# One plan for all engines, and a first block of tokens that takes all twelve weight columns in one pass

## The chip, the core and the metric

The kernel runs on one core of a Trainium2 chip. The core has a matrix engine (TensorE, PE in the profile, with its weight loads as PEld), a vector engine (VectorE, DVE), an engine for functions and copies (ScalarE, ACT), a general engine (GpSimd, POOL) and an engine whose queue issues the DMAs (SyncE, SP). Each works through its own queue in order and waits for the others by semaphores. SBUF is the memory on the chip; matmuls write into eight banks of PSUM. The metric is the device time of one execution in microseconds.

## The reference

Three layers in a row, in float32, on 4 x 768 = 3072 tokens of 384 channels (8 heads of 48). First a gated linear attention, then a product of two projections, then a mixture of four experts:

```python
f = 1.0 / (1.0 + np.exp(-f_logit))
for t in range(S):                       # S = 768, for each batch and head
    state = f[..., t, :, None] * state + k[..., t, :, None] * v[..., t, None, :]
    y[..., t, :] = q[..., t, :] @ state
x = ((y @ w_a) * (y @ w_b)) @ w_out      # 384 -> 1536 -> 384
p = domain_probs / (domain_probs.sum(-1, keepdims=True) + 1e-09)
out = sum(p[:, e:e + 1] * (np.maximum(x @ w1[e], 0.0) @ w2[e]) for e in range(4))
```

The weights `w_a`, `w_b` and `w_out` arrive as float64; all else is float32.

## The kernel before

`phase_a` (line 132) does attention and the second layer, `phase_b` (line 508) the experts. A third part, `general`, is a fallback for inputs outside the limits that `flags` watch; it does not run here.

**Attention** goes in 24 steps of 128 tokens for one batch: step `s` is piece `s // 4` of batch `s % 4`, and four steps make one block of 512 tokens. A step loads f, k, q and v (`a_load`), turns the gates into running products R (`a_exp`, `a_scan`), scales q and k by them (`a_hat`), transposes k (`a_trans`), forms scores and masks them (`a_scores`), and adds up outputs and the state for the step four later (`a_out`). For the first eight steps (`EARLY`, line 31) 1/R comes from Ln and Exp on ScalarE with a correction; for the others from four reciprocals on VectorE (`a_inv`). In the early steps one of the two masks is a copy on ScalarE and a select on GpSimd. The outputs are split into a rounded part and a remainder, `xT`, so that a float32 product is three fast matmuls.

**Weights of the second layer**: 18 units of 128 x 768 numbers, three for every two of the twelve columns (128 wide) of the hidden layer: `w_a` and `w_b` of one column, `w_out` of two, the two projections of the other column. As float64 they arrive as pairs of 32-bit words, 768 KB each (`fetch_w`). `to_f32` (line 97) makes float32 of the words: one pass of ScalarE (line 103) and six of VectorE (lines 104 to 116), the first of them a clamp. `split` then rounds a weight on ScalarE and leaves the remainder to GpSimd.

**The second layer** goes in units, one column for one block of tokens: `half` twice (nine matmuls each), a copy of the first half, the product of both on VectorE, split in two parts, and `outp`, the last product, which adds nine matmuls into three banks. In the first eight units (`WHOLE`) the product and the weight are not split, and `outp` is six instructions of the slower full form. From unit `LATE` = 20 VectorE makes the remainders, before that GpSimd. `outp` stands one unit behind. The first two columns of the first block are done in halves of 256 tokens.

**The order.** Units run over columns 0 to 8 for block 0, the same for block 1, then columns 9 to 11 for block 0 and for block 1 (`H1` = 9, line 459), then all twelve for blocks 2 to 5. Each block's three banks are emptied into `x2raw` at the end of a part; the second part's are added to it there. Attention and conversions are strung between the units by hand (`attn_to`, `conv_to`, from line 403), with fractions of a list of operations due by a unit. The framework's scheduler may still move instructions of one engine, except those that `kept` pins, which are matmuls of blocks 2 to 5. `busy` (line 177) writes filler matmuls on a tile of zeros, 104 in all, between the matmuls of the first four steps.

Of the kernel before, what the change touches and what calls it, by code (L numbers as in the profile page):

```python
# [21 lines left out]
C = 128  # L22
# [8 lines left out]
EARLY = 2 * B  # L31

SLOTS = 11
FREE = 3 * B
LEAD = 2
OUTPOS = 4
AHEAD = 2
GRP = 2
BUSY = (8, 10, 8, 6)
H1 = 9  # L40
NSUB = 2
CA = 2
FRAC = 0.4
WHOLE = 8
LATE = 20
LIMIT = float(2.0 ** 60)
# [6 lines left out]
def gla_moe_moe_kernel(ctx: ExitStack, tc, qkf, vv, wab, wout, w12, probs, gq, gv, gp, out):  # L53
# [12 lines left out]
    def bank(tag, bufs=None, name=None):  # L66

        i = turn.get(tag, 0)
        turn[tag] = i + 1
        return banks8[WHERE[tag][i % len(WHERE[tag])]]  # L70
# [9 lines left out]
    flags = const.tile([128, NSTEP, 3], F32, tag="flags", name="flags")  # L80
    junk = const.tile([128, 1, 128], BF16, tag="junk", name="junk")
# [15 lines left out]
    def to_f32(raw, w=None):  # L97
# [5 lines left out]
        nc.scalar.activation(out=mag, in_=high.bitcast(F32), func=AF.Abs)  # L103
        nc.vector.tensor_scalar(out=mag, in0=mag, scalar1=F64_ZERO, scalar2=F64_INF, op0=ALU.max, op1=ALU.min)
        mag_i, val_i = mag.bitcast(U32), val.bitcast(U32)
        nc.vector.tensor_scalar(
            out=mag_i, in0=mag_i, scalar1=5, scalar2=2, op0=ALU.logical_shift_left, op1=ALU.logical_shift_right
# [24 lines left out]
    def phase_a(actx):  # L132
        ws = actx.enter_context(tc.tile_pool(name="ws", bufs=1))
# [4 lines left out]
        w_f, raws = {}, {}  # L138
# [3 lines left out]
        w_pair = [None]  # L142


        def w_fetch(u):
            f, i = 2 * (u // 3), u % 3
            raws[u] = fetch_w(wout[f // 2] if i == 1 else wab[f + i // 2])

        def w_ready(u):
            f, i = 2 * (u // 3), u % 3  # L150
            raw = raws.pop(u)
            if i == 1:
                dst = wo_all[:, f:f + 2].rearrange("p f c -> p (f c)")
                if wide:
                    to_f32(raw, dst)
                else:
                    nc.scalar.copy(out=dst, in_=raw)
                return
            f += i // 2
            w = to_f32(raw) if wide else raw  # L160
            if f == 0:
                w_pair[0] = wts.tile([128, 2, 2, 2 * DM], F32R, tag="x", name="w01", bufs=1)
            t = w_pair[0][:, f] if f < 2 else wts.tile([128, 2, 2 * DM], F32R, tag="w", name="w")
            split(nc.gpsimd, t[:, 0], t[:, 1], w)
            w_f[f] = t.rearrange("p a (i k c) -> p a i k c", i=2, k=KC)


        T, st_t, xT = {}, {}, {}

        fixed = [False]  # L170

        def kept(ins):

            if fixed[0]:
                tc.keep_in_program_order(ins)

        def busy(n):

            if n:
                b = bank("o")  # L180
                for _ in range(n):
                    nc.tensor.matmul(b, junk[:, 0], junk.to_broadcast([128, 4, 128]), start=True, stop=True)
# [4 lines left out]
        def a_load(s):  # L187
            t = {}
            early = wts.tile([128, 3, 4, C], F32, tag="w", name="qkf") if s < B else None
            for i, name in ((2, "f"), (1, "k"), (0, "q")):  # L190
                t[name] = slot(name) if early is None else early[:, i]
                nc.sync.dma_start(out=t[name], in_=qkf[s, i])
            t["v"] = slot("v").rearrange("p j c -> p (j c)") if early is None else v_early[:, s * 512:(s + 1) * 512]
            t["v"] = t["v"].rearrange("p (h e) -> p h e", h=H)
            nc.sync.dma_start(out=t["v"], in_=vv[s])
            T[s] = t

        def a_exp(s):
            u = T[s]["f"]
            nc.scalar.activation(out=u, in_=u, func=AF.Exp, scale=-1.0)  # L200
            nc.scalar.activation(out=u, in_=u, func=AF.Identity, bias=1.0)
            nc.scalar.activation(out=cap[:, :, 0:1], in_=u[:, :, 0:1], func=AF.Copy)
            T[s]["R"] = slot("R")

        def a_scan(s):

            u, R = T[s]["f"], T[s]["R"]
            flat = [x.rearrange("p j c -> p (j c)") for x in (R, u, cap)]
            nc.vector.tensor_tensor_scan(  # L209
                out=flat[0], data0=flat[1], data1=flat[2], initial=1.0, op0=ALU.mult, op1=ALU.min  # L210
            )

        def a_inv(s, j):
            if s >= EARLY:
                nc.vector.reciprocal(out=T[s]["f"][:, j], in_=T[s]["R"][:, j])  # L215

        def a_hat(s):

            t = T[s]
            R, q, k, p = t.pop("R"), t["q"], t["k"], t.pop("f")  # L220
            end = slice(C - 1, C)
            pe = at.tile([128, 4, 1], F32, tag="pe", name="pe", bufs=3)
            t["pe"] = pe
            j1 = at.tile([128, 4, C], BF16, tag="j", name="j")
            if s >= EARLY:
                nc.gpsimd.tensor_tensor(out=k, in0=k, in1=R, op=ALU.mult)  # L226
                nc.scalar.activation(out=j1, in_=q, func=AF.Square, accum_out=flags[:, s, 1:2])
                nc.vector.tensor_reduce(out=flags[:, s, 0:1], in_=R[:, :, C - 1], axis=AX.X, op=ALU.max)
                nc.vector.tensor_tensor(out=q, in0=q, in1=p, op=ALU.mult)
                nc.vector.tensor_copy(out=pe, in_=p[:, :, end])  # L230
            else:
                nc.scalar.activation(out=p, in_=R, func=AF.Ln)
                nc.scalar.activation(out=p, in_=p, func=AF.Exp, scale=-1.0)
                nc.gpsimd.tensor_tensor(out=k, in0=k, in1=R, op=ALU.mult)
                nc.scalar.activation(out=j1, in_=q, func=AF.Square, accum_out=flags[:, s, 1:2])
                nc.vector.tensor_reduce(out=flags[:, s, 0:1], in_=R[:, :, C - 1], axis=AX.X, op=ALU.max)
                nc.vector.scalar_tensor_tensor(out=q, in0=q, scalar=-1.0, in1=p, op0=ALU.mult, op1=ALU.mult)
                nc.gpsimd.tensor_tensor(out=R, in0=R, in1=p, op=ALU.mult)
                nc.vector.scalar_tensor_tensor(out=q, in0=R, scalar=-2.0, in1=q, op0=ALU.add, op1=ALU.mult)  # L239
                nc.vector.scalar_tensor_tensor(  # L240
                    out=pe, in0=R[:, :, end], scalar=-2.0, in1=p[:, :, end], op0=ALU.add, op1=ALU.mult
                )
            j2 = at.tile([128, 4, C], BF16, tag="j", name="j")
            nc.scalar.activation(out=j2, in_=k, func=AF.Square, accum_out=flags[:, s, 2:3])

        def a_trans(s):

            t = T[s]
            if s // B == NC - 1:
                return  # L250
            kps = bank("k")
            for j in range(4):
                kept(nc.tensor.transpose(kps[:, j * C:(j + 1) * C], t["k"][:, j], ident))
            if s < B:
                busy(BUSY[1])
            t["kt"] = slot("kt")
            nc.scalar.copy(out=t["kt"].rearrange("p j c -> p (j c)"), in_=kps)

        def a_scores(s):
            t = T[s]  # L260
            q, k = t["q"], t.pop("k")
            sps = [bank("s"), bank("s")]
            for j in range(4):
                for h in range(2):
                    r = 64 * h
                    kept(nc.tensor.matmul(  # L266
                        sps[h][:, j * C:(j + 1) * C], k[r:r + D, j], q[r:r + D, j], start=True, stop=True
                    ))
            if s < B:
                busy(BUSY[2])  # L270
            t["s"] = []
            for h in range(2):
                m = slot("ss")
                if h and s < EARLY:
                    nc.scalar.copy(out=m.rearrange("p j c -> p (j c)"), in_=sps[h])
                    nc.gpsimd.affine_select(
                        out=m, in_=m, compare_op=ALU.is_ge, fill=0.0, base=0, pattern=[[0, 4], [1, C]],
                        channel_multiplier=-1,
                    )
                    t["s"].append(m)  # L280
                    continue
                nc.vector.tensor_tensor(
                    out=m,
                    in0=sps[h].rearrange("p (j c) -> p j c", j=4),
                    in1=mask.rearrange("p (o c) -> p o c", o=1).to_broadcast([128, 4, C]),
                    op=ALU.mult,
                )
                t["s"].append(m)

        def a_out(s):  # L290
# [32 lines left out]
            if s < B:  # L323
                busy(BUSY[3])
# [478 lines left out]
```

## Time and profile before

| | |
|---|---|
| median of 3 runs | 1416.17 us (1415.77 to 1416.61) |
| the profiled execution | 1415.95 us |
| its span, first to last instruction | 1414.2 us |
| PE busy in the span | 1381.6 us, 98%, 7599 instructions |
| DVE busy | 583.2 us, 41%, 880 instructions |
| ACT busy | 392.9 us, 28% |
| POOL busy | 191.3 us, 14% |

The page's slices show the engines unevenly loaded: forty slices of 35 us, each digit the busy share in tenths. DVE stands at 7 to 9 for the first five slices and at 2 for the last twenty-odd; PE is at 7 and 8 in the first three and at 9 after them. A share over the whole span says little here; the views are read by stretch. Times in timelines are counted from the start of the span.

### The profile page before, as it was taken

What the parts mean: (1) busy time and instruction counts of PE and PEld (TensorE: products, weight loads), DVE (VectorE), ACT (ScalarE), POOL (GpSimd) and SP (SyncE); (2) the same over time, 40 slices, a digit from 0 to 9 for tenths busy, and PEclk for the clock granted to TensorE, in tenths of its full rate; (3) what the DMA queues carried; (4) which work ended last, traced back from release to release, by engine and by line L of the source; (5) the groups of instructions that cost most, each with busy time, mean ns of one, the idle gap of its engine ahead of it and who ended that gap; (6) DMA issues with size and microseconds to landing.
All of it is one profiled execution on the core that took longest, in us unless ns stands there. A gap on an engine that the chain in (4) does not pass through costs nothing.

```text
span 1414.2 us, 18060 instructions
## 1 busy us (share of the span) xinstructions
PE 1381.6 (98%) x7599; PEld 1190.7 (84%) x7599; DVE 583.2 (41%) x880; ACT 392.9 (28%) x733; POOL 191.3 (14%) x128
## 2 busy tenths in 40 slices
PE   7889999999999999999999999999999999999998
PEld 4676787888888878889999989999989999989997
DVE  7899716856565654432222222222222222222222
ACT  6453334433333324341111211111311112111111
POOL 4334431100000002360000310000300002100000
PEclk9889999999999999999999999999999999999999
DMA  6544101222121101200000200000200001000001
GB/s 232 168 156 147 53 0 44 67 65 57 32 66 45 56 17 35 68 23 0 1 1 0 68 23 1 0 1 1 89 1 0 1 0 45 1 23 23 23 23 47
DMA packets 28168, 60.27 MB, mean 43 GB/s; under 512 B 4016, under 2 KB 9392, under 8 KB 28080
## 3 DMA queue, kind: packets, MB, share of 16 engines
q1 hardware_dynamic: 28080, 59.05, 13.3%
q8 instruction: 61, 1.00, 0.3%
q14 instruction: 27, 0.22, 0.0%
HBM read 51.95 MB, written 4.72 MB: 40 GB/s over the span
## 4 chain that ended last, share of the span: by engine, by line


## 5 line engine op out<-in xcount | busy, mean ns | idle before, releaser
L545 PE MATMUL bank<-w,h 128*128 128x384 f32 x2304 | 411.3, 335 | 0.0
L545 PEld LDWEIGHTS bank<-w,h 128*128 128x128 f32 x2304 | 402.8, 188 | 5.0
L527 PE MATMUL bank<-x,w 128*128 128x512 f32 x1728 | 404.8, 390 | 0.0
L527 PEld LDWEIGHTS bank<-x,w 128*128 128x128 f32 x1728 | 323.3, 188 | 65.2
L530 DVE SCALAR_TENSOR_TENSOR h<-bank,h 128x512 fp32r<-128x512 f32 x192 | 132.7, 691 | 533.1 <-ACT h L529 533.1
L358 PE MATMUL bank<-xT,w 128*128 128x512 f32 (+1 forms) x1332 | 319.1, 390 | 3.4 <-DVE ab L494 1.6
L358 PEld LDWEIGHTS bank<-xT,w 128*128 128x128 f32 x1332 | 246.2, 190 | 57.7 <-DVE ab L494 2.4
L529 ACT ACTIVATE h<-bank 128x512 fp32r<-128x512 f32 x192 | 114.9, 598 | 616.0 <-PE bank L527 516.7
L376 PE MATMUL bank<-hl,wo 128*128 128x512 f32 x594 | 148.9, 394 | 1.6 <-DVE hl L122 1.1
L122 POOL TENSOR_TENSOR w<-raw,w 128x768 fp32r<-128x768 f32 x32 | 59.0, 1844 | 575.6 <-ACT w L121 573.6
L376 PEld LDWEIGHTS bank<-hl,wo 128*128 128x128 f32 x594 | 109.9, 188 | 27.3 <-DVE hl L122 1.8
L494 DVE TENSOR_TENSOR ab<-bank,a 128x512 f32<-128x512 f32 x66 | 45.0, 682 | 132.7 <-PE bank L358 132.7
L121 ACT CAST hl<-ab 128x512 fp32r<-128x512 f32 x66 | 40.9, 620 | 83.5 <-DVE ab L494 83.5
L555 DVE SCALAR_TENSOR_TENSOR acc<-bank,pr,acc 128x384 f32<-128x384 f32 x72 | 39.5, 610 | 58.6 <-PE bank L545 58.6
L486 ACT COPY a<-bank 128x512 f32<-128x512 f32 (+1 forms) x74 | 42.1, 569 | 70.0 <-PE bank L358 70.0
L122 DVE TENSOR_TENSOR hl<-ab,hl 128x512 fp32r<-128x512 f32 x54 | 49.4, 914 | 28.6 <-ACT hl L121 28.6
L215 DVE RECIPROCAL f<-R 128x128 f32<-128x128 f32 x64 | 57.6, 926 | 0.7
L226 POOL TENSOR_TENSOR k<-k,R 128x512 f32<-128x512 f32 x16 | 22.0, 1373 | 265.6 <-DVE R L209 247.0
L121 ACT CAST wo<-wo_all 128x384 fp32r<-128x384 f32 x66 | 33.9, 515 | 40.0 <-PE bank L376 39.2
L122 DVE TENSOR_TENSOR wo<-wo_all,wo 128x384 fp32r<-128x384 f32 x54 | 34.4, 637 | 19.1 <-ACT wo L121 19.0
L121 ACT CAST w<-raw 128x768 fp32r<-128x768 f32 x32 | 26.8, 837 | 44.7 <-PE bank L545 30.8
L266 PE MATMUL bank<-q,k 48*128 48x128 f32 x320 | 25.6, 296 | 6.5 <-DVE q L239 5.8
(106 smaller groups left out, 773.0 us busy)
## 6 DMA issues: line engine op xcount, KB each, us to landing
raw<-in_w_dram SPq DMA_DIRECT2D x32, 384.0 KB, 3.0
raw<-in_wab_dram SPq DMA_DIRECT2D x12, 768.0 KB, 4.9
f<-in_qkf_dram SPq DMA_DIRECT2D x20, 256.0 KB, 2.7
k<-in_qkf_dram SPq DMA_DIRECT2D x20, 256.0 KB, 2.7
q<-in_qkf_dram SPq DMA_DIRECT2D x20, 256.0 KB, 2.8
v<-in_v_dram SPq DMA_DIRECT2D x20, 256.0 KB, 3.0
raw<-in_wout_dram SPq DMA_DIRECT2D x6, 768.0 KB, 4.4
out_dram<-acc SPq DMA_DIRECT2D x24, 192.0 KB, 1.9
```

Of the source, the lines that this page charges most:

```text
L121: nc.scalar.copy(out=hi, in_=x)
L122: engine.tensor_tensor(out=lo, in0=x, in1=hi.bitcast(F32), op=ALU.subtract)
L215: nc.vector.reciprocal(out=T[s]["f"][:, j], in_=T[s]["R"][:, j])
L358: kept(nc.tensor.matmul(p, l, r, start=m == 0, stop=m == len(ops) - 1))
L376: kept(nc.tensor.matmul(banks[m][:, o:o + n], w[:, a, m * 128:(m + 1) * 128], hl[:, b], start=f == fs[0] and q == 0 and o == 0, stop=f == ...
L486: nc.scalar.copy(out=a, in_=pa)
L494: nc.vector.tensor_tensor(out=ab, in0=pb, in1=a, op=ALU.mult)
L527: nc.tensor.matmul(p, l, r, start=i == 0, stop=i == len(ops) - 1)
L529: nc.scalar.activation(out=h[:, 0], in_=p, func=AF.Relu)
L530: nc.vector.scalar_tensor_tensor(out=h[:, 1], in0=p, scalar=0.0, in1=h[:, 0].bitcast(F32), op0=ALU.max, op1=ALU.subtract)
L545: nc.tensor.matmul(src, h[:, b, t * 128:(t + 1) * 128], w2[e, f][:, a], start=f == 0 and q == 0, stop=f == NF2 - 1 and q == 2,)
L555: nc.vector.scalar_tensor_tensor(out=dst, in0=src, scalar=p, in1=dst, op0=ALU.mult, op1=ALU.add)
```

## The change

The string of operations written by hand goes. In its place every operation of `phase_a` becomes a `Node`: an engine, a cost in us, what it comes after, which buffers it takes and gives back. The nodes are written in an order that a simulation in the kernel's own Python finds before anything runs: a pass backwards gives each node its distance to the end, then a pass forwards takes, engine by engine, the most urgent node that can start within 0.3 us of the earliest. Each instruction is then pinned in that order on its engine (`pin`). With it come other changes:

- Units run over all twelve columns for block 0, then all twelve for block 1 (`ORDER`). No block has two parts any more, so no sums are added in `x2raw`.
- The conversion has no clamp. VectorE's shift reads the high words where they lie, every second word of the raw tile. ScalarE runs Abs and then Exp over the raw words with running sums into `wseen`, which a few small operations after `phase_a` turn into the flag that the clamp stood for.
- `EARLY` is 12 and not 8 steps; the first four steps have both masks on VectorE; `WHOLE` is 10 units and not 8.
- The load of the probabilities comes after the fourth step. Squares for the flags come after the scores.
- Filler matmuls are written where the plan has PE idle, and only ahead of the first last product.

The diff, cut to its core:

```diff
-EARLY = 2 * B
+EARLY = 3 * B
...
-BUSY = (8, 10, 8, 6)
-H1 = 9
-CA = 2
-FRAC = 0.4
-WHOLE = 8
+ORDER = ((0, 12, 0), (0, 12, 1))
+WHOLE = 10
 LATE = 20
+
+T_FIRST, STRETCH, SLACK, PATIENCE, HOP, DMA_LAG = 32.0, 1.15, 1.0, 0.3, 0.06, 2.0
...
+        class Node:
+            def __init__(self, eng, cost, fn, after=(), take=(), give=(), late=None):
...
+        full_room = {"t": SLOTS, "k": 6, "w": 10, "x": 1, "xT": 2, "st": B + 1, "pe": 3, "a": 1, "ab": 1, "hl": 2,
+                     "wo": 2, "b5": 1, "b6": 1, "b7": 1, "h": 2, "o": 1}
...
+            n_f = Node("SP", 2.0 if wide else 1.0, fetch, fetched[-1:] + [conv_mid[-2]], take=["k"])
...
+                    nc_op = nc.vector.tensor_scalar(
+                        out=box["mag"].bitcast(U32), in0=box["high"], scalar1=5, scalar2=2,
+                        op0=ALU.logical_shift_left, op1=ALU.logical_shift_right,
+                    )
...
+                    return nc.scalar.activation(
+                        out=box["sq"], in_=box["raw"][:, :, 1].bitcast(F32), func=AF.Abs, accum_out=seen[:, 0:1]
+                    )
...
+                    return nc.scalar.activation(
+                        out=box["sq"], in_=box["sq"], func=AF.Exp, scale=-64.0 / F64_ZERO, accum_out=seen[:, 1:2]
+                    )
...
+                n_s = Node("ACT", 2.2, lambda: (pin(sums()), pin(exps())), [n_f])
+                n1 = Node("DVE", 0.8, shift, [n_f, conv_end[-2]], take=["k"])
...
+                conv_mid.append(Node("free", 0.0, None, [n4, n_s], give=["k"]))
...
+            n6 = Node("ACT", 0.83, hi, [n_w] + ([w_n[0]] if ff == 1 else []),
+                      take=["x"] if ff == 0 else [] if ff == 1 else ["w"])
+            w_n[ff] = Node("POOL", 2.0, lambda: nc.gpsimd.tensor_tensor(
+                out=box["t"][:, 1], in0=w(), in1=box["t"][:, 0].bitcast(F32), op=ALU.subtract), [n6], give=back)
...
+            gate = [out_n[s - 2], up_n.get(s - 2)] if s >= B else []
...
+            if s < EARLY and not first:
+                def copied():
+                    t["s", 1] = slot("ss")
+                    return act.copy(out=t["s", 1].rearrange("p j c -> p (j c)"), in_=t["sb"][1])
...
+            else:
+                n_m.append(Node("DVE", 0.69, lambda: masked(1), [n_s], take=["t"], give=["b7"]))
...
+            ready = [w_n[f]] + [mv_n[s] for s in range((i * NB + o) // C, (i * NB + o + n) // C)]
+            cost = 9 * (n + 34) / 2400
+            n_a = Node("PE", cost, lambda: half(0), ready + [state["b"]], take=["h"])
...
-        parts = [full[:H1], full[H1:]]
-        order = [(i, fs) for fs in parts for i in range(2)] + [(i, full) for i in range(2, NBLK)]
+        order = [(i, full[a:b]) for a, b, i in ORDER] + [(i, full) for i in range(2, NBLK)]
...
+        pr_n = Node("SP", 0.2, lambda: nc.sync.dma_start(out=pr, in_=probs), [mv_n[B - 1]])
...
+            eng = min(best, key=lambda q: (min(best[q])[0], q))
+            t0 = min(best[eng])[0]
+            start, _, _, x, need = min((c for c in best[eng] if c[0] <= t0 + PATIENCE), key=lambda c: (c[1], c[2]))
...
+            if eng == "PE" and first_op not in end:
+                idle = start - free_at.get(eng, 1.0)
+                for _ in range(int(max(0.0, idle - 0.1) / 0.22)):
+                    pin(nc.tensor.matmul(
+                        banks8[2], junk[:, 0], junk.to_broadcast([128, 4, 128]), start=True, stop=True
+                    ))
+            free_at[eng] = start + x.cost
+            ins = x.fn()
+            if eng != "PE" and ins is not None and not isinstance(ins, tuple):
+                pin(ins)
```

## Rows read from the trace of the kernel before

**Rows 1.** Busy time by stretch: stretch, length, each engine's busy us and instructions, clock, DMA.
```profile
core 0: us, PE busy (x) PEld busy (x) DVE busy (x) ACT busy (x) POOL busy (x), PEclk, DMA share, GB/s
0.00:149.28 149.28, 128.14 (x848) 91.55 (x849) 133.43 (x183) 76.13 (x151) 62.38 (x48) 0.91 0.51 172
38.79:149.28 110.49, 97.26 (x641) 74.37 (x640) 104.18 (x139) 51.76 (x101) 47.00 (x30) 0.89 0.48 156
149.28:1414.00 1264.72, 1253.49 (x6752) 1099.19 (x6750) 449.73 (x697) 316.81 (x582) 128.88 (x81) 1.00 0.09 27
```

**Rows 2.** The same view, VectorE's work on the conversions' tile `cv` alone.
```profile
core 0: us, DVE busy (x), PEclk, DMA share, GB/s
0.00:149.28 149.28, 80.28 (x90) 0.91 0.51 172
```

**Rows 3.** Timeline of TensorE (start, busy us, line, operands): last products and halves of units.
```profile
116.37 2.74 PE L369 MATMUL bank<-hl,wo_all 128*128 128x512 f32 x6
118.54 4.84 PE L358 MATMUL bank<-xT,w 128*128 128x512 f32 x18
...
185.93 2.20 PE L376 MATMUL bank<-hl,wo 128*128 128x512 f32 x9
187.97 4.24 PE L358 MATMUL bank<-xT,w 128*128 128x512 f32 x18
192.05 2.20 PE L376 MATMUL bank<-hl,wo 128*128 128x512 f32 x9
```

**Rows 4.** VectorE's groups by line up to 149.28: count, busy us, mean ns, idle before.
```profile
L104 DVE TENSOR_SCALAR cv<-cv 128x768 f32<-128x768 f32 x15 | 11.7, 777 | 0.4 <-ACT cv L103 0.4
...
L209 DVE TENSOR_TENSOR_SCAN R<-f,cap 128x512 f32<-128x512 f32 x5 | 6.0, 1210 | 0.0
...
L282 DVE TENSOR_TENSOR ss<-bank,mask 128x512 f32<-128x512 f32 x8 | 5.4, 678 | 0.2 <-PE bank L266 0.2
...
L215 DVE RECIPROCAL f<-R 128x128 f32<-128x128 f32 x4 | 3.8, 938 | 0.0
...
L230 DVE COPY pe<-f 128x4 f32<-128x4 f32 x1 | 1.3, 1261 | 0.0
...
L561 DVE TENSOR_SCALAR prs<-prs 128x24 f32<-128x24 f32 x1 | 0.9, 905 | 0.0
```

**Rows 5.** Timeline of VectorE and GpSimd around one late shift of line 106.
```profile
114.20 0.55 DVE L106 TENSOR_SCALAR cv<-cv 128x768 uint32<-128x768 uint32 x1
...
115.14 0.95 DVE L109 SCALAR_TENSOR_TENSOR cv<-raw,cv 128x768 uint32<-128x768 uint32 x1
115.16 2.60 POOL L122 TENSOR_TENSOR w<-cv,w 128x768 fp32r<-128x768 f32 x1 [2.02 <-ACT w L121]
116.01 2.17 DVE L106 TENSOR_SCALAR cv<-cv 128x768 uint32<-128x768 uint32 x1
```

**Rows 6.** Groups by line up to 149.28: ScalarE and GpSimd.
```profile
L122 POOL TENSOR_TENSOR w<-cv,w 128x768 fp32r<-128x768 f32 x10 | 20.6, 2059 | 22.8 <-ACT w L121 22.8
...
L103 ACT ACTIVATE cv<-raw 128x768 f32<-128x768 f32 x15 | 13.6, 905 | 20.7 <-DVE cv L113 20.7
...
L121 ACT CAST w<-cv 128x768 fp32r<-128x768 f32 x10 | 8.3, 827 | 3.8 <-DVE cv L116 3.8
...
L244 ACT ACTIVATION_READ_ACCUMULATOR j<-k 128x1 f32 x5 | 0.9, 188 | 0.0
```

**Rows 7.** Busy time by stretches of 20 us (columns as in rows 1).
```profile
60.00:80.00 20.00, 19.56 (x146) 17.07 (x146) 17.38 (x27) 9.18 (x18) 6.78 (x4) 0.69 0.42 132
80.00:100.00 20.00, 15.56 (x121) 12.86 (x122) 20.00 (x26) 9.86 (x20) 8.14 (x7) 0.74 0.52 170
180.00:200.00 20.00, 20.00 (x90) 16.53 (x90) 2.77 (x4) 5.78 (x10) 7.29 (x8) 1.00 0.00 1
```

**Rows 8.** Timeline of TensorE: three waits, in square brackets with what ended them.
```profile
60.33 1.64 PE L266 MATMUL bank<-q,k 48*128 48x128 f32 x10 [3.89 <-DVE q L239]
...
161.39 0.32 PE L310 MATMUL bank<-ss,v 128*64 128x128 f32 x1 [1.20 <-DVE ss L282]
...
228.10 3.70 PE L358 MATMUL bank<-xT,w 128*128 128x512 f32 x15 [0.84 <-POOL w L122]
```

**Rows 9.** The page's DMA issues: count, KB each, us to landing.
```profile
raw<-in_wab_dram SPq DMA_DIRECT2D x12, 768.0 KB, 4.9
```

**Rows 10.** Busy time by stretch, the filler matmuls' tile `junk` alone.
```profile
core 0: us, PE busy (x) PEld busy (x) DVE busy (x), PEclk, DMA share, GB/s
38.79:149.28 110.49, 5.32 (x21) 1.61 (x19) 0.00 (x0) 0.89 0.48 156
```

More of the change, by code (lines that the diff above doesn't have):

```diff
@@ L168, in phase_a, with fetch @@
[L168 to L182, printed above, removed]
+            out_w = i == 1
+            ff = f + i // 2
+            box = {}
+            def fetch():
+                src = wout[f // 2] if out_w else wab[ff]
+                if wide:
+                    box["raw"] = keep.tile([128, 2 * DM, 2], U32, tag="k", name="raw")
+                    return nc.sync.dma_start(
+                        out=box["raw"], in_=src.bitcast(U32).rearrange("p (n t) -> p n t", t=2)
+                    )
+                box["raw"] = keep.tile([128, 2 * DM], F32, tag="k", name="raw")
+                return nc.sync.dma_start(out=box["raw"], in_=src)
@@ L194, in a_load @@
[L194 to L211, printed above, removed]
@@ L246, in a_trans @@
[L246 to L288, printed above, removed]
@@ new lines, in step_plan, with trans, kt @@
+            Node("free", 0.0, None, [n_pe, n_q, n_k, n_max], give=["t"] if first else ["t", "t"])
+            gap = [up_n.get(s - 1), out_n.get(s - 1)]
+            n_kt = None
+            if not last:
+                def trans():
+                    t["kb"] = bank("k")
+                    for j in j_of:
+                        pin(nc.tensor.transpose(t["kb"][:, j * C:(j + 1) * C], t["k"][:, j], ident))
+                def kt():
+                    t["kt"] = slot("kt")
+                    return act.copy(out=t["kt"].rearrange("p j c -> p (j c)"), in_=t["kb"])
+                n_t = Node("PE", 0.65, trans, [n_k, lo_n.get(s - 1)] + gap + ([] if early else [n_q]), take=["b5"])
+                n_kt = Node("ACT", 0.59, kt, [n_t], take=["t"], give=["b5"])
@@ new lines, in token_lo @@
+            def token_lo():
+                x = xT[i][:, :, :, o:o + C]
+                return dve.tensor_tensor(
+                    out=x[:, 1], in0=t["y"].rearrange("p (j c) -> p j c", j=4), in1=x[:, 0].bitcast(F32), op=ALU.subtract
+                )
+            n_x = Node("ACT", 0.59, token_hi, [n_o] + [x_first.get(i)], take=["xT"] if new_x else [])
+            if new_x:
+                x_first[i] = n_x
+            n_x = Node("DVE", 0.69, token_lo, [n_x], give=["b5"])
+            lo_n[s] = n_x
@@ L395, in phase_a @@
+            done = Node("free", 0.0, None, ends, give=["o"] if o + n == NB else [])
+            state["raw"][i] = done
+        used = {}
         make_identity(nc, ident)
@@ L439, in phase_a, with pin @@
[L439 to L455 removed]
+        def pin(ins):
+            return tc.keep_in_program_order(ins)
@@ new lines, in phase_a @@
+        n = None
+        for o in range(0, NB, HB):
+            n = Node("ACT", 0.85, lambda o=o: split_0(o, 0), [state["raw"][0], ahead, n], take=["x"] if o == 0 else [])
+            Node("POOL", 2.0, lambda o=o: split_0(o, 1), [n])
+        rows[-1][2].append(last_op[0])
+        first_op = rows[1][2][0]
+        clock = T_FIRST
+        spread = {}
+        for a_n, b_n, op_n in rows:
+            for x in (a_n, b_n, *op_n):
+                spread[x] = clock
+                clock += x.cost * STRETCH
```

644 lines of the change are left out of this document (415 added, 229 removed).

## The prediction, made before the changed kernel was built or run

> **What bounds the kernel now.** I read busy time by stretch first [rows 1]. From 149.28 us on TensorE (PE) is busy 1253.5 of 1264.7 us: there only PE's own work counts, and the change takes hardly any of it away. Up to 149.28 PE is busy 128.1 of 149.3. VectorE (DVE) is busy 133.4 of those 149.3, and 104.2 of the 110.5 between 38.79 (first matmul of the first unit) and 149.28 (first matmul of the second block of tokens). So the time of this kernel is the moment at which DVE has prepared enough for PE to go on without waits, plus PE's work from there. Last I asked what DVE does up to 149.28 [rows 2]: 15 of the 18 weight conversions, six operations each, keep it busy for 80.3 us. The rest is attention and the units' products.
>
> **The point to compare.** A unit (one column block for one block of tokens) costs PE 6.12 us when nothing waits, from one last product to the next, 185.93 to 192.05 [rows 3]. Before enters the second block of tokens at 149.28 with nine columns of the first done; the change enters it with twelve. In PE work, before stands at that point at 149.28 + 3 x 6.12 = 167.6 us. From there both have the same work to the end, so the change gains 167.6 minus its own start of the second block (call it T), and some small terms. The rivals differ in T or in what follows it.
>
> **The change part by part.**
>
> *The conversion* loses the clamp of line 104, 0.78 us each, 0.70 without the 0.08 by which neighbours on DVE overlap [rows 4, 5], and keeps five operations: 80.3 - 15 x 0.70 = 69.8, or 4.65 each. T needs all 18: 83.7, which is 3.4 more than before had done. The shift of line 106 now reads the raw words, every second of 4 bytes, where it read a packed copy. No row shows a one-input operation on that layout. The nearest are line 106 itself, 0.55 alone, and line 109, which reads the same strided words and a second input, 0.95 alone [rows 5]. Nothing suggests less than 0.55, so it is 0 to 0.4 each, 0 to 7.2 in all. I take 0, by line 106, the same operation with one input. The Trainium skill, "VectorE: DVE Perf Modes", section "What auto-detection actually checks", lets a single 32-bit source in SBUF keep the doubled rate without asking for a step of one; by it the term is 0 too. No run here shows it yet.
>
> *ScalarE (ACT)* gets two passes over each weight, Abs and Exp, where it had one of 0.905, and a reading of the accumulator behind each, 0.19 as behind the squares [rows 6]: 18 x 2.19 = 39.4 against 13.6, some 26 us more. ACT is busy 76.1 of 149.3 [rows 1], so about 102 of some 155: hidden in its idle time. If that cover were gone, one pair ahead of a needed copy would cost up to 2.2.
>
> *Attention and products.* The first four steps get both masks on DVE, and lose a copy on ACT and a select on GpSimd (POOL): 4 x 0.68 = 2.7 more for DVE. Three more columns need three products of the same shape, 3 x 0.68 = 2.0 [rows 4]. Of step 8, due only for the third block, before did the scan, four reciprocals and the copy of the end ahead of 149.28: 1.2 + 3.8 + 1.3 = 6.3 [rows 4]; I move that behind T. Steps 8 to 11 turn from reciprocals to Ln and Exp there, where DVE is busy 2.8 of 20 us [rows 7]: nothing on the path. The sums of probabilities, 0.9 for the longest [rows 4], wait for a load that now comes after the fourth step: behind T as well.
>
> *Sum on DVE:* 133.4 + 3.4 + 2.7 + 2.0 - 6.3 - 0.9 = 134.3 busy, 141.5 with the dear shift. With the same 15.9 us of idle time that is 150.2 to 157.4.
>
> *The tail.* In before the weights run ahead of the units. Now the last column's conversion is among DVE's last work, and behind it stand ACT's rounding, 0.83, POOL's remainder, 2.06 [rows 6], and the unit's two halves, 192.05 - 187.97 = 4.08 [rows 3]: 7.0 in all if the conversion is the very last, 0 if attention of steps 6 and 7 comes behind it. I take 7, as the column is wanted just before T. So T = 157.2, and the gain 10.4.
>
> *PE.* Units 8 and 9 now multiply by unsplit weights: 2.17 (116.37 to 118.54) against 2.04 (185.93 to 187.97) for the last product [rows 3], + 0.3 for two. The wait of 0.84 on a late weight at 228.10 [rows 8] goes: - 0.8. The filler matmuls are now written only where the plan sees PE idle before the first product; they lie in PE's waits then and now: 0. The partial sums that are spared are a dozen short operations on DVE and ACT, in a stretch where both idle: 0.
>
> *Queues.* Every engine is now pinned to the plan's order. On SyncE's queue a weight is fetched once the conversion two before it has read its raw words; behind it stand the next loads of attention. A raw weight lands in 4.9 us [rows 9], while DVE spends 134.3 / 18 = 7.5 us for each weight with all that comes between: covered. If it weren't, each late one would cost up to 4.9 of DVE.
>
> *Total.* The profiled execution took 1415.95 us, 1414.2 of span and 1.75 around it, 0.2 under the median of the runs. 1415.95 - 10.4 + 0.3 - 0.8 = 1405.0, and 1405 against the median too. With the dear shift, or with no tail, it is 1412 or 1398.
>
> **The rivals.**
>
> *PE stays as badly fed as before: slower.* Between 38.79 and 149.28 PE loses 13.2 us idle [rows 1], 5.3 in fillers [rows 10] and 0.11 x 110.5 = 12.2 by a granted clock of 0.89 [rows 1]: after 3.89 us of nothing at 56 us the mean clock is 0.69 from 60 to 80, and 0.74 from 80 to 100 [rows 7, 8]; the level below 2.4 GHz is 1.2. That leaves 79.8 us of work, a share of 0.72. The change has 79.8 + 18.4 = 98.2 to do. At 0.72 that takes 136, T is 175, and the time 1423. For it: each column now wants 1.5 conversions (7.0) and a product of DVE while PE needs 6.12 and its part of a step, so a gap comes back with every column, and behind the first product no fillers are written. Against: before had one column more in store at 149. It decides where PE's share falls below 98.2 / 128.8 = 0.76. The Trainium skill, "TensorE: Matmul & The Clock Gate", has the clock cut when TensorE idles and given back under sustained work; the rows agree.
>
> *The gain is given back later: near no change.* The plan orders every engine by fixed durations. If at 8 to 16 of the 16 later steps PE waits as at 161.39, 1.20 [rows 8], that is 10 to 19: 1415 to 1424. Against: from 149.28 on DVE is busy only 450 of 1265 [rows 1], and before too keeps a written order there, with few waits.
>
> *DVE is freed from POOL: much faster.* Line 106 takes 0.55 alone, and 2.17 when it meets an operation of POOL that began at 115.16 [rows 5]. The Trainium skill, "SBUF — State Buffer", section "Who interferes with whom", describes an exclusive lock on a pair of ports that these two share; the row agrees. If the plan keeps them apart, a conversion is two of 0.55 and three of 0.95, less 0.08 each: 3.55, 18 are 64, 19.7 less: T 137.5, time 1385. Against: POOL has about the same 62 us of work in the same stretch [rows 1], and the plan knows nothing of their meeting.
>
> **How the numbers follow.** Forecast 0.52 (1398 to 1412); badly fed 0.17 (1423); given back 0.19 (two thirds of it within 1413 to 1419, the rest above); freed 0.12 (1385 and up). A measurement of this kernel can tell some 0.2% from no change, 2.8 us: faster is under 1413.3, slower over 1419. Faster 0.52 + 0.12 = 0.64; same 0.13; slower 0.17 + 0.06 = 0.23. The range of 1390 to 1423 holds the forecast, nearly all of the given-back case, half of the badly fed and the near part of the freed one: 0.8.
>
> **What would show it.** T near 157 (175 in the slow rival, 138 in the fast); DVE busy up to T for 134 to 142 us; the shift at 0.55 or at 0.95 alone; the granted clock between the first unit and T; PE's idle time behind T, 11 us in before, over 20 if the gain is given back. A conversion far from 4.65 us, or a DVE that idles much more than 16 us before T, would make the prediction wrong.

## The result, and the profile after

The changed kernel takes 1425.2 us (median, 1420.31 to 1428.4) against 1416.04 (1415.31 to 1417.06): ratio 1.0057, 95% interval 1.0046 to 1.0067. It is 9 us slower where 11 faster were forecast, and outside the range. The profiled execution took 1425.2, with a span of 1423.5 us.

First busy time by stretch of the changed kernel, as in [rows 1] (stretch, length, then each engine's busy us), split where the second block of tokens begins. That is 178.19: fourteen units belong to block 0 (two columns in halves, ten whole), and VectorE's fourteenth product is the one at 176.42. Where an expectation below says 180, it counts from the unit's second group of matmuls.

```profile
core 0: us, PE busy (x) PEld busy (x) DVE busy (x) ACT busy (x) POOL busy (x), PEclk, DMA share, GB/s
0.00:178.19 178.19, 158.58 (x973) 108.16 (x974) 148.75 (x189) 99.82 (x204) 67.30 (x50) 0.94 0.40 138
34.34:178.19 143.85, 131.61 (x786) 93.53 (x787) 121.88 (x157) 76.20 (x157) 53.49 (x34) 0.94 0.37 124
178.19:1423.50 1245.31, 1237.59 (x6687) 1083.15 (x6685) 418.77 (x654) 320.23 (x587) 123.53 (x79) 1.00 0.09 29
...
34.34:88.92 54.58, 46.42 (x290) 31.31 (x290) 48.25 (x63) 27.33 (x57) 11.72 (x6) 0.93 0.50 176
88.92:178.19 89.27, 85.19 (x496) 62.22 (x497) 73.63 (x95) 48.86 (x100) 41.77 (x28) 0.94 0.28 93
```

By T, the start of the second block, nearly everything is said. T is 178.2; the break-even was 167.6. That is 10.6 too late, and the span is 9.3 longer. Behind T PE is idle for 7.7 us, less than in before [rows 1], so nothing is lost there. Ahead of T VectorE is busy for 148.75 us and idle for 29.4. The last two rows part the way to T: from 88.92 on PE is idle for only 4.1 of 89.3 us. Most of what PE loses lies ahead of that: 8.2 us of idle time, and all of the 23.8 us of fillers behind the start of the first unit.

Next, TensorE's timeline (start, busy us, line, operands; in brackets the wait before it and what ended it), with two products of VectorE.

```profile
34.34 4.08 PE L500 MATMUL bank<-xT,w 128*128 128x256 f32 x18 [0.46 <-DMA xT<-xT]
...
49.36 1.33 PE L500 MATMUL bank<-xT,w 128*128 128x256 f32 x9
50.54 17.23 PE L724 MATMUL bank<-junk 128*128 128x512 bf16 x79
71.78 6.06 PE L500 MATMUL bank<-xT,w 128*128 128x256 f32 x36 [4.02 <-DVE hl L516]
...
88.92 10.09 PE L500 MATMUL bank<-xT,w 128*128 128x512 f32 x36 [4.05 <-DVE hl L516]
...
113.50 0.60 PE L342 MATMUL bank<-ident,k 128*128 128x128 f32 x4
114.03 1.16 PE L355 MATMUL bank<-q,k 48*128 48x128 f32 x16
...
128.27 0.60 PE L342 MATMUL bank<-ident,k 128*128 128x128 f32 x4
...
144.87 0.60 PE L342 MATMUL bank<-ident,k 128*128 128x128 f32 x4
...
158.64 0.63 PE L342 MATMUL bank<-ident,k 128*128 128x128 f32 x4 [0.19 <-DVE xT L436]
...
178.19 4.24 PE L500 MATMUL bank<-xT,w 128*128 128x512 f32 x18
```
```profile
71.32 0.41 DVE L516 TENSOR_TENSOR hl<-bank,a 128x256 f32<-128x256 f32 x1
...
176.42 0.69 DVE L521 TENSOR_TENSOR ab<-bank,a 128x512 f32<-128x512 f32 x1 [2.39 <-PE bank L500]
```

Before, the first and the last of the four transposes:
```profile
55.83 0.60 PE L253 MATMUL bank<-ident,k 128*128 128x128 f32 x4
...
103.19 0.60 PE L253 MATMUL bank<-ident,k 128*128 128x128 f32 x4
```

Two things stand out. The first unit's sums are ready at 38.4, but VectorE forms their product only at 71.32; until then they hold one of the two banks for halves. The first half of the next unit runs in the other one at 49.36; its second half has to wait until 71.78, and PE runs 79 filler matmuls and waits for 4 us (below: the hole). And attention's steps 4 to 7, whose tokens the second block needs, start their transposes at 113.50, 128.27, 144.87 and 158.64; before had them at 55.83, 75.25, 88.22 and 103.19.

Last, the pieces of the conversion: VectorE on the tile `cv` as in [rows 2], the shift alone as in [rows 5], ScalarE's pair as in [rows 6].

```profile
0.00:178.19 178.19, 84.43 (x90) 10.00 (x12) 25.19 (x12) 0.94 0.40 138
```
```profile
8.54 0.56 DVE L207 TENSOR_SCALAR cv<-raw 128x768 uint32<-128x768 uint32 x1 [2.06 <-DMA raw<-in_wab_dram]
```
```profile
L215 ACT ACTIVATE j<-raw 128x768 bf16<-128x768 f32 x18 | 16.4, 911 | 8.9 <-DMA raw<-in_wab_dram 8.9
L220 ACT ACTIVATE j<-j 128x768 bf16<-128x768 bf16 x18 | 15.2, 843 | 0.6
L215 ACT ACTIVATION_READ_ACCUMULATOR j<-raw 128x1 f32 x18 | 3.5, 193 | 0.0
L220 ACT ACTIVATION_READ_ACCUMULATOR j<-j 128x1 f32 x18 | 3.4, 186 | 0.0
```

All as forecast: 84.4 against 83.7, 0.56 against 0.55, a pair of 2.14 against 2.19.

### The profile page after: what moved, and what is told of

The parts are those of the page before. It is cut to its first block, busy times and chain, and to the rows that moved or that the text cites. A ratio compares the mean times of both kernels' runs of the same rounds, so it can differ in the third digit from the quotient of the medians.

```text
span 1423.5 us, 18221 instructions
## 1 busy us (share of the span) xinstructions
PE 1396.2 (98%) x7659; PEld 1191.3 (84%) x7659; DVE 567.5 (40%) x843; ACT 420.0 (30%) x791; POOL 190.8 (13%) x128
## 4 chain that ended last, share of the span: by engine, by line
## 5 line engine op out<-in xcount | busy, mean ns | idle before, releaser
L500 PE MATMUL bank<-xT,w 128*128 128x512 f32 (+1 forms) x1332 | 319.9, 394 | 11.2 <-DVE hl L516 9.5
L500 PEld LDWEIGHTS bank<-xT,w 128*128 128x128 f32 x1332 | 248.1, 193 | 66.3 <-DVE hl L516 10.6
L552 PE MATMUL bank<-hl,wo 128*128 128x512 f32 x576 | 142.4, 393 | 0.0
L309 POOL TENSOR_TENSOR k<-k,R 128x512 f32<-128x512 f32 x20 | 27.1, 1355 | 255.2 <-DVE R L302 227.4
L724 PE MATMUL bank<-junk 128*128 128x512 bf16 x170 | 41.4, 400 | 1.6 <-DVE junk L81 1.6
L330 DVE RECIPROCAL f<-R 128x128 f32<-128x128 f32 x48 | 42.5, 923 | 0.3
```

What stands on the lines that cost most here:

```text
L330: n = Node("DVE", 0.93, lambda j=j: dve.reciprocal(out=t["f"][:, j], in_=t["R"][:, j]), [n])
L500: pin(nc.tensor.matmul(p, l, r, start=m == 0, stop=m == len(ops) - 1))
L552: pin(nc.tensor.matmul(banks[m][:, o:o + n], t["w"][:, a, m * 128:(m + 1) * 128], t["hl"][:, b], start=f == fs[0] and q == 0 and o == 0, s ...
L724: pin(nc.tensor.matmul(banks8[2], junk[:, 0], junk.to_broadcast([128, 4, 128]), start=True, stop=True))
```

## The experiments

Four theories of the late T. *Products*: the plan puts products off, and PE stands still behind the held bank. *Steps*: the plan puts steps 4 to 7 off, and the second block waits for them. *Order*: twelve columns at once cost by themselves, without any plan. *Work*: they need so much of VectorE ahead of T that it is late in any plan; this one came last, after the first three had been tried.

**Products first** (theory *products*).
```diff
+        products = []     # the node of every L516 and L521 product is put in
             x.late = -back[x]
+        for x in products:
+            x.late -= 1e6
```


> The changed kernel with one difference: in the plan VectorE's products of the units, which give back the two banks of a unit's halves, are taken as soon as they can start, ahead of conversions. Theory A (in the plan the first units' products stand on VectorE behind 20 us of conversions, so TensorE finds no bank and stops): the second unit's second half comes at some 52 us and not 71.8, the wait and most of the 79 fillers go, the second block starts at 157 to 163 and not 180, and the time falls from 1425 to 1403 to 1409. Rival B (twelve columns in one pass want more conversions than VectorE can give): the hole only moves to later columns, the second block still starts after 173, and the time stays within 1418 to 1428.


Measured: 1423.32, 1.0044 [1.0028, 1.0061]. TensorE's timeline:
```profile
34.36 4.18 PE L501 MATMUL bank<-xT,w 128*128 128x256 f32 x18 [0.47 <-DMA xT<-xT]
...
52.06 2.49 PE L501 MATMUL bank<-xT,w 128*128 128x256 f32 x18
...
165.15 1.09 PE L342 MATMUL bank<-ident,k 128*128 128x128 f32 x4 [4.67 <-DVE xT L436]
...
178.94 3.23 PE L501 MATMUL bank<-xT,w 128*128 128x512 f32 x13 [1.27 <-DMA xT<-xT]
```
The hole goes (second unit at 52), yet T stays at 178.9, now waiting for the tokens of steps 6 and 7. The theory *products*, by itself, falls.

**The old order of columns in the plan** (nine columns, second block, the other three).
```diff
-ORDER = ((0, 12, 0), (0, 12, 1))
+ORDER = ((0, 9, 0), (0, 9, 1), (9, 12, 0), (9, 12, 1))
```


> The changed kernel with its plan, but the units in the order of before: columns 0 to 8 for the two blocks, then 9 to 11 for both, with partial sums. Theory A: the early hole is there all the same, as it lies in the first columns, and the time stays at 1418 or more. Rival B: without the demand for columns 9 to 11 in the first pass the time is that of before or better, 1405 to 1416.


Measured: 1423.7, 1.005 [1.0033, 1.0066]. The same hole is there, and steps 4 to 7 at 88.86 to 137.92. The order alone does not mend the plan.

**Both of these edits.**


> Both: products ahead of conversions, and the units in the order of before. Theory A: near the first of these runs, 1402 to 1410, as the order of columns matters little. Rival B: the best of the three by 10 us or more.


Measured: 1419.05, 1.002 [1.001, 1.003]. Here the second block starts at 143.5, ahead of before's 149.28, and the kernel is still 2.5 us slower. So with the old order T no longer tells the end: time is lost behind it. First before, then this run, up to 220 us:
```profile
149.28:220.00 70.72, 68.86 (x362) 56.72 (x361) 29.50 (x41) 25.25 (x51) 27.80 (x22) 1.00 0.06 15
```
```profile
143.47:220.00 76.53, 72.23 (x363) 58.51 (x364) 40.45 (x58) 32.91 (x67) 36.52 (x29) 0.96 0.15 53
```
PE idles for 4.3 us there against 1.9, and the clock of 0.96 takes some 3 more. That is about 5.5 of the 7.1 us that the profiled execution loses behind T.

**The hand order with twelve columns** (theory *order*): before, one constant.
```diff
-H1 = 9
+H1 = 12
```


> The kernel before, its hand-written order kept, with twelve columns in one pass for the first block and then the second, no partial sums. Theory A: the order of columns alone costs little; VectorE has the clamp still, so 18 conversions are 3 x 5.4 = 16 us more work before the second block, which starts at 165 to 172: 1414 to 1421. Rival B: as slow as the change or slower, 1423 to 1432.


Measured: 1422.74, 1.0044 [1.0028, 1.0061].
```profile
157.42 2.35 PE L358 MATMUL bank<-xT,w 128*128 128x512 f32 x9 [3.31 <-DVE ab L494]
...
179.53 2.65 PE L358 MATMUL bank<-xT,w 128*128 128x512 f32 x11
```
With no plan, the hand-written order, the steps early as ever and the old conversion, T is 179.5. In the hand order the order of columns alone brings two thirds of the loss. VectorE is busy for 154.7 us up to there.

**Steps 4 to 7 and products first**; **steps 4 to 7 alone** (theory *steps*); **both with the old order**.
```diff
                 step_plan(s_next)
+                if B <= s_next < 2 * B:
+                    steps.extend(nodes[n0:])     # n0: len(nodes) ahead of step_plan
...
+        for x in steps:
+            x.late -= 5e5
```


> The changed kernel, twelve columns in one pass, with the products first as in the first run and the operations of attention steps 4 to 7 ahead of the conversions too. In the change and in the first run the transposes of steps 4 to 7 come at 108 to 113, then every 15 us, and the second block starts 22 us after the last; in before they come at 55.8, 75, 88 and 103. Theory C (the plan lets the conversions go first and so begins the four steps, which follow one another, 50 us too late): the transposes of step 4 come at 50 to 65, the second block starts at 158 to 168, the time is 1403 to 1413. Rival B (18 conversions in one pass are too much work, whatever the order on VectorE): the conversions now come late, TensorE waits for weights, the second block starts after 172, the time is 1416 to 1425, near the twelve columns in the hand-written order, 1422.7.

> The changed kernel with the operations of attention steps 4 to 7 ahead of the conversions, but the products where the change has them. Theory C: most of the gain, 1405 to 1415, as the second block waits for the steps. Rival A2 (late products and late steps each cost the same 10 us and only both together give it back): 1418 to 1425.

> As the run with both ahead, with the order of columns of before (0 to 8 for two blocks, then 9 to 11). Theory C: the order of columns matters little once the plan serves the steps: within 4 us of that run. Rival B: 6 us or more below it, under 1412.


Measured: both, 1418.81, 1.002 [1.001, 1.003], T 171.05; steps alone, 1425.34, 1.0065 [1.0048, 1.0082], T 181.15, with the waits for products of up to 5.8 us; both with the old order, 1421.13, 1.0033 [1.0022, 1.0045]. Neither fault alone is enough, and both mended give 6 us back. But the steps came early only in part. TensorE, then VectorE, with both first:
```profile
59.72 0.60 PE L342 MATMUL bank<-ident,k 128*128 128x128 f32 x4
...
113.82 1.16 PE L355 MATMUL bank<-q,k 48*128 48x128 f32 x16
```
```profile
112.35 0.16 DVE L324 SCALAR_TENSOR_TENSOR pe<-R,qkf 128x4 f32<-128x4 f32 x1
112.54 0.36 DVE L471 SCALAR_TENSOR_TENSOR st<-bank,pe 128x192 f32<-128x192 f32 x1
```
Step 4's transposes stand at 59.72, its scores at 113.82. Scores are planned behind the state of the step before, and that waits for an operation of 0.16 us on four numbers a row, which the plan left until 112.35, as it does in the changed kernel (112.86).

**Before with the new conversion only**: the change's five operations on VectorE and its two passes on ScalarE, with the flag that hangs on them.
```diff
-        nc.scalar.activation(out=mag, in_=high.bitcast(F32), func=AF.Abs)
-        nc.vector.tensor_scalar(out=mag, in0=mag, scalar1=F64_ZERO, scalar2=F64_INF, op0=ALU.max, op1=ALU.min)
...
-            out=mag_i, in0=mag_i, scalar1=5, scalar2=2, op0=ALU.logical_shift_left, op1=ALU.logical_shift_right
+            out=mag_i, in0=mag_i if seen is None else high, scalar1=5, scalar2=2,
...
+            nc.scalar.activation(out=sq, in_=high.bitcast(F32), func=AF.Abs, accum_out=seen[:, 0:1])
+            nc.scalar.activation(out=sq, in_=sq, func=AF.Exp, scale=-64.0 / F64_ZERO, accum_out=seen[:, 1:2])
```


> The kernel before with the conversion of the change alone: no clamp on VectorE, the shift on the raw words, two passes with sums on ScalarE. VectorE saves 15 x 0.70 = 10.5 us up to the second block. If VectorE's load sets the start of the second block there, as the prediction has it: 1406 to 1412. Rival (waits in the chains of attention set it, or the two passes on ScalarE stand in the way of needed copies): 1414 to 1421.


Measured: 1416.8, 1.0008 [0.9998, 1.0017]: no change.
```profile
0.00:148.74 148.74, 125.95 (x849) 89.55 (x849) 125.60 (x168) 90.20 (x196) 62.88 (x49) 0.94 0.51 172
```
VectorE is busy 125.6 us up to T, 7.8 less than before [rows 1], and T is 148.74, 0.5 earlier. Its idle time took the rest: 23.1 us against 15.9. So in before the cheaper conversion gains nothing. That VectorE's work as such does not set T there is likely, but not shown by this run alone: ScalarE has 14.1 us more to do up to T. VectorE waits for ScalarE no longer than before (7.0 us, 7.6 in before), but longer for GpSimd (7.9, 2.9 in before), and TensorE waits 6.4 us for masks that GpSimd selects from ScalarE's copies, where before had no such wait. Whether ScalarE's new passes hold up these masks I have not separated.

**The held-up scale first as well**: products, steps 4 to 7, and of steps 0 to 3 the scale and the state; then the same without the products, and with the old order.
```diff
+            if first:
+                steps.append(n_pe)
...
+                if first:
+                    steps.append(n)      # n: the node of the state
```


> Products and steps 4 to 7 come first as in the run with both, and now also two operations of steps 0 to 3: the scale of 128x4 (0.16 us) and the state that it makes. In the run with both, the scale of step 3 was written at 112.35 us though its input was there some 60 us before, and the scores of step 4, which need that state, stood at 113.82 though their queries were ready at 72.2. Theory 'the chain of steps sets the second block, and this one small operation holds its head': scores of step 4 near 60 to 75 instead of 113.8, steps 5 to 7 some 30 to 40 us earlier, the second block at 155 to 164 instead of 171.05, and 1408 to 1415. Rival 'the conversions set it': the steps come earlier but the second block stays within 3 us of 171, and 1417 to 1420.

> Only steps 4 to 7 and the scale and state of steps 0 to 3 come first; the products stay where the plan has them. Theory 'two separate faults, each of which can hold TensorE': the steps' scores come at 60 to 80, but the product of the first unit still comes some 30 us after its sums, so the second block comes between the run with both (171.05) and the changed kernel (178.2), and 1418 to 1424. Rival 'the scale was the whole fault': 155 to 166, and 1408 to 1415.

> As the run with products, steps and scale first, with nine columns, the second block, then the other three, as the kernel before has it. Theory 'twelve columns at once cost nothing once the steps are early, as the second block waits for them alone': within 3 us of the run with twelve. Theory 'the order of columns costs by itself, since three more weights must be converted ahead of the second block': this one is 4 to 8 us faster than it, 1404 to 1410; the second block at 140 to 146.


Measured: 1420.77, 1.0041 [1.0025, 1.0057], T 177.9; without the products first 1424.73, 1.0062 [1.0048, 1.0077], T 179.0; with the old order 1419.94, 1.0028 [1.0016, 1.004]. TensorE in the first of these:
```profile
62.90 1.16 PE L357 MATMUL bank<-q,k 48*128 48x128 f32 x16
...
94.09 0.63 PE L344 MATMUL bank<-ident,k 128*128 128x128 f32 x4 [2.11 <-DVE xT L438]
...
149.16 0.73 PE L505 MATMUL bank<-xT,w 128*128 128x512 f32 x2 [1.19 <-ACT w L250]
151.07 5.48 PE L505 MATMUL bank<-xT,w 128*128 128x512 f32 x16 [1.17 <-POOL w L254]
...
167.43 0.73 PE L505 MATMUL bank<-xT,w 128*128 128x512 f32 x2 [2.18 <-ACT w L250]
169.70 6.32 PE L505 MATMUL bank<-xT,w 128*128 128x512 f32 x16 [1.54 <-POOL w L254]
```
The scores of step 4 come at 62.9, 51 us earlier, and the last transposes at 94. What the theory *steps* asks for is there in full, and T is where it was in the changed kernel: now the last columns wait for their weights. What went ahead took VectorE's time from the conversions: up to 94 us they have 32.3 us of it, in the changed kernel 48.1. So it falls as the cause of the late T; the steps were one queue among several for the same engine.

The four runs with the old order also bear on the theory *order*. Against the same plan with twelve columns, the old order changes the median by -1.5 us (no other edit), -4.3 (products first), +2.3 (products and steps) and -0.8 (scale too). So the 6 us that twelve columns cost in the hand order are not simply won back in the plan; the causes overlap, and their prices can't be added up.

**Two operations less in each conversion**, in the changed kernel and in the run with all put first (theory *work*).
```diff
-                n3 = Node("DVE", 0.72, ...)      # the mask
-                n4 = Node("DVE", 1.0, ...)       # times the low word
```


> The changed kernel with two of the five VectorE operations of each conversion left out, the mask and the product with the low word, so the weights are wrong: 18 x (0.66 + 1.01) = 30 us less work for VectorE, and the plan is made with that. Theory 'VectorE's work sets the second block' (about 150 us of it must be done first in every version with twelve columns): the second block at 148 to 158 instead of 178.2, and 1396 to 1406. Rival 'the order of the plan sets it' (put-off products, steps and scales, engines that wait for one another): the second block stays at 170 or later, most of the 30 us turns into idle time of VectorE, and 1416 to 1425.

> The run with products, steps and scales first, with the same two operations of each conversion left out. There the steps are done by 103 us and the last four weights come late, while VectorE stands idle for 27 us, partly behind products that wait for TensorE, which waits for the weights. Theory 'VectorE's work sets the second block': 145 to 155 instead of 177.9, and 1393 to 1403. Rival 'VectorE and TensorE wait for one another in their written orders': it falls by less than half of the 30 us, to 163 or later, and 1406 to 1418.


Measured: 1392.53, 0.9835 [0.9819, 0.9851]; 1409.78, 0.9962 [0.9947, 0.9976]. Busy time by stretch, first the changed kernel with light conversions, then the other:
```profile
0.00:146.26 146.26, 131.61 (x874) 93.54 (x875) 119.49 (x153) 98.39 (x204) 66.20 (x50) 0.98 0.49 168
...
146.26:1391.60 1245.34, 1237.59 (x6687) 1083.06 (x6685) 418.77 (x654) 320.35 (x587) 123.57 (x79) 1.00 0.09 29
```
```profile
0.00:162.30 162.30, 138.05 (x899) 99.77 (x900) 123.63 (x160) 101.76 (x209) 70.43 (x52) 0.94 0.46 161
```
In the changed kernel VectorE loses 29.3 us of work, T falls by 31.9 (178.19 to 146.26), the kernel by 32.7, and behind T the two kernels agree to 0.03 us. T falls by more than the work, and for a reason: the plan was made anew with the lighter conversions, and the hole went too. VectorE's first product of this run, then the fillers from the first unit to T in the changed kernel and here:
```profile
43.87 0.41 DVE L510 TENSOR_TENSOR hl<-bank,a 128x256 f32<-128x256 f32 x1
```
```profile
34.34:178.19 143.85, 23.78 (x107) 10.21 (x107) 0.00 (x0) 0.94 0.37 124
```
```profile
31.97:146.26 114.29, 1.47 (x6) 0.51 (x6) 0.00 (x0) 0.97 0.46 156
```
So 22 of the 32 us are fillers that are gone, and this run does not tell what the work alone is worth. With products, steps and scale first, the hole is smaller (10.2 us of fillers, 1.7 with the light conversion). There VectorE loses 27.2 us of work, T falls by 15.6, and VectorE's idle time grows from 27.1 to 38.7. By the medians that kernel gains 11.0 us, less than half of the work, as the rival of its expectation had it. So the theory *work* holds in part: with twelve columns VectorE's work is one cause of the late T, worth some 0.4 to 0.6 us for each us of it where products and steps are put first (a plan made anew there too). That it sets T one for one is not shown.

All versions with twelve columns side by side, from their profiled executions (us; "behind T" is the span less T). Each row is one execution: that with steps and products first is 2.1 us under the median of its version, that with the scale too 3.3 above.

```
                                  T      span    behind T  DVE busy, idle up to T
changed kernel                  178.19  1423.5   1245.3     148.8   29.4
products first                  178.94  1422.4   1243.5     153.8   25.2
hand order, twelve columns      179.53  1421.9   1242.4     154.7   24.9
steps and products first        171.05  1415.0   1244.0     151.7   19.3
steps first                     181.15  1425.4   1244.3     153.9   27.3
products, steps, scale first    177.92  1422.2   1244.3     150.8   27.1
steps, scale first              179.03  1423.3   1244.3     153.5   25.5
changed, light conversion       146.26  1391.6   1245.3     119.5   26.8
all first, light conversion     162.30  1407.5   1245.2     123.6   38.7
```

The column "behind T" stays within 3 us while T moves by 35: with this order of columns nearly the whole difference lies ahead of T. And each version with the full conversion has 149 to 155 us of VectorE's work ahead of it.

## Why the prediction was wrong

- **The point to compare** was right within 4 us. Before has 1414.2 - 167.6 = 1246.6 behind its break-even, the versions with twelve columns 1242.4 to 1245.3.
- **The conversion** was right, at 84.4 us, with the cheap shift. The Trainium skill, "VectorE: DVE Perf Modes", section "What auto-detection actually checks", asks of a single source that it lie in SBUF, and not for a step of one; this is borne out here: a source with a step of two words ran at 0.56 us, the packed one at 0.55.
- **ScalarE's pair** was hidden, nearly as said: between the first unit and T PE never waits for ScalarE, and VectorE waits for it for 9.5 us up to T (7.6 in before). Raw weights landed in 5.5 us (4.9 before), and VectorE waited for them for 3.0 us in all.
- **Given back later** did not happen: 7.7 us of idle PE time behind T, fewer than before's 11.2.
- **The step that failed** is "With the same 15.9 us of idle time that is 150.2", with the sum of 134.3 ahead of it. Measured: 148.8 busy and 29.4 idle. In this count the tail of 7 is part of the idle time. So 157.2 became 178.2: 14.4 from busy, 13.5 from idle, less 7.0.
  - *Busy, 14.4 too low.* By lines up to T: the nine scales of 128x4 took 6.2 us (1.2 for eight in before), the scaling of queries 22.6 for nine steps (17.9 for eight), the scans 12.0 (I had left 9.7). Step 8, which I had moved behind T, was ahead of it after all, since T itself came later. Of the other 2.4, the conversions are 0.7 (84.4 for 83.7), and four small operations on the flags of the weights, which the sum did not have, another 0.7 (from 143.39). The rest I have not split.
  - *Idle, 13.5 too low.* I took before's idle time as a property of the work. It belongs to the order of the work: the same engine idles 15.9 us in before, 23.1 in before with the new conversion, 19.3 to 29.4 in the versions with twelve columns and the full conversion. Between the first unit and T VectorE waits 10.3 us for PE before products (2.4 in before), and from 165 to T it is busy only 5.2 of 13.2 us, with the last column on PE. These last 8.0 us stand where the forecast had its tail of 7.0, but the path that it priced is not there: the last conversion ends at 157.9, 20 us before T, and PE is idle for only 2.5 us from then on.

```profile
165.00:178.19 13.19, 13.19 (x75) 10.47 (x74) 5.16 (x8) 5.49 (x12) 5.62 (x6) 0.89 0.07 15
```

- **The trap in the reasoning.** I read VectorE's 133 of 149 us as "VectorE sets T", and so counted what the cheaper conversion saves as gain. In before that saving gained nothing: 7.8 us less work moved T by 0.5. With twelve columns, which want 1.5 conversions for each further column within the same stretch, VectorE's work does count, but 27.2 us less of it moved T by 15.6 with products and steps first. The rest went into idle time. So a busy share of 90% did not say what a saved microsecond is worth, in either kernel.
- **The rival that came true** in its number is "PE stays as badly fed as before", T 175 and 1423, given 0.17. Its sum holds: between the first unit and T PE is busy 131.6 of 143.9 us, of which 23.8 are fillers (5.3 in before), and the clock of 0.94 takes another 8.6. The 99.2 left (98.2 forecast) are 0.69 of the stretch, under the 0.76 from which it decides. Its mechanism holds only in part: it saw a gap come back with every column, but all fillers and two thirds of the idle time lie ahead of 88.92, mostly in the one hole of the first product. So some luck is in its number. The argument against it, one more column in store at 149, did not carry: with twelve columns the hand order itself, store and all, came to T at 179.5.
- **Open.** Which share of the late T each cause has: the order of columns, VectorE's work and the plan's order overlap, and the hand order with twelve columns was not run with the new or the light conversion. Steps and products first came to T at 171 and the same with the scale early at 178, but 5 of these 7 us lie between the two executions that were profiled: the medians are 2.0 apart. And what the plan costs with the old order of columns: there T was ahead of before's by up to 6 us in three of four runs (143.5, 144.4, 148.0), and those kernels were 2.5 to 5 us slower. Between T and 220 us their PE idles for 4.3, 9.3 and 3.6 us (1.9 in before) at clocks of 0.96, 0.95 and 0.98; why, I have not followed. No version beat before, except the two that leave work out.

## What to carry to other kernels

An engine that is 90% busy ahead of a milestone isn't yet the bound of it: take some work from it, keep the order of the rest, and see whether the milestone moves or the idle time grows. Where a plan is made anew for the lighter work, as here, both change at once. Idle time up to a milestone belongs to the order of the work, so a new order needs its own estimate of it, not the old one's. A plan by longest path that knows the buffers only when it places an operation put off short operations here that free a bank or hold a chain (a product of 0.41 us by 33 us, a scale of 0.16 us to the head of a chain of four steps), and mending one of them moved the wait to the next.

## What the runs showed of the hardware

**A tiny operation beside GpSimd.** A scale of 128x4 takes 0.15 us alone; beside an operation of GpSimd it took eight times as long, VectorE and GpSimd of the changed kernel:
```profile
120.23 1.56 POOL L320 TENSOR_TENSOR R<-R,f 128x512 f32<-128x512 f32 x1 [2.86 <-DVE flags L307]
120.59 1.23 DVE L324 SCALAR_TENSOR_TENSOR pe<-R,f 128x4 f32<-128x4 f32 x1
```
It ends with GpSimd's operation (121.79 and 121.82). The Trainium skill, "SBUF — State Buffer", section "Who interferes with whom", tells of an exclusive lock on the ports that the two share; this row agrees, and another, where the scale ended with GpSimd's operation too (161.26 and 161.24):
```profile
158.99 2.25 POOL L254 TENSOR_TENSOR w<-cv,w 128x768 fp32r<-128x768 f32 x1
159.50 1.76 DVE L324 SCALAR_TENSOR_TENSOR pe<-R,f 128x4 f32<-128x4 f32 x1
```
So in these two rows the price went by what was left of GpSimd's operation, and not by the size of VectorE's.

**TensorE's clock** follows the waits, as in [rows 7]: after the wait of 4.05 us at 88.92 the granted clock is 0.58 up to 93.0 and 1.00 from there, and a run of 36 matmuls took 10.09 us; the same kind of run at 102.32, at 1.00, took 8.77.

**The spread.** The changed kernel's runs lie 8 us apart (1420.31 to 1428.4), before's 1.8. The mean granted clock goes along: 0.994 for the three shortest, 0.989 for the longest. Why this kernel meets more of it is not shown.
